# First batch of a chunked attention with a mixture of experts: two heads in one product, loads in halves, no limit on transfers, a new order

## The chip, the cores and the metric

The kernel runs on one core of one Trainium2 chip. The metric is the time of one execution on the device in microseconds (us); lower is better. A core has five engines, each with its own instruction stream: TensorE (PE; its weight loads are shown apart as PEld), VectorE (DVE), ScalarE (ACT), GpSimd (POOL) and SyncE (SP), which here only issues transfers between DRAM and the core's memory (SBUF). PE writes its results to PSUM.

## What is computed

```
for c in range(S // 32):                       # chunks of 32 queries
    ctx = positions 32*c-16 .. 32*c+40         # 16 to the left, 8 to the right, cut at the ends
    k_full = concat(mem_k, k[ctx]);  v_full = concat(mem_v, v[ctx])     # 8 memory keys
    a = softmax(q_c @ k_full.T / 8)
    out[c] = a @ v_full
x = out as (4*768, 512)
for e in range(4):
    y += p[:, e] * (relu(x @ w1[e]) @ w2[e])   # p: domain_probs, each row divided by its sum
```

There are 4 batches of 8 heads, 768 positions and 64 values a head. All is float32. A product of the experts is made of three products of split operands (a high part and a low remainder); a product of the attention is a plain float32 product.

## The kernel before, in words

A unit u is 96 queries (three chunks) of all 8 heads; a batch has 8 units. The first batch is worked before the experts can begin, since the first expert's first product needs x. Everything after it is one long stretch of expert products, with the attention of later units between them.

Units 0 to 3 of the first batch go one at a time, by these steps, whose names are used below:

- S: `early_scores` (L1411) loads `qk[u]` (128 rows of 3712 bytes: two heads by 64 values in the rows) and makes the scores. A product has 64 rows of contraction (one head), 32 queries and 64 keys. There are 24 of them a unit: 4 head pairs, 3 chunks and 2 heads of the pair (the `rows` slice, L531). The chunk chooses a strip of 32 columns of PE's array, the head one half of its rows. DVE then takes the maximum (L1426), subtracts it (L1456), and ACT takes the exponential (L607).
- T: `early_turn` transposes the result on PE in four transposes (L1499); the result is copied to `aTs` (two buffers).
- X: `early_values` loads `v0[u]` (128 rows of 3120 bytes) and multiplies, 24 products of 64 by 32 by 65 (L1520); the 65th column is the sum of the weights. DVE inverts it and multiplies (L1531 to L1535).
- Y: `early_mix` transposes the result (L1552), ACT copies the high part into `xa` (L603), DVE or POOL makes the low part.

Units 4 to 7 go in pairs: P4 and P6 (`early_pair`, L1476; two halves a and b on PE) and then X4 to X7. N0 to N7 are the first products of the first expert (`plain_first`, L931); each needs all of Y0 to Y3 and a weight block loaded from `w1`.

The order is written out by hand. `FIRST_BLOCK` makes the steps; `Plan.follow` puts their operations into the order of `FIRST_ORDER`, and every engine's stream is in that order. `MID_ORDER` and `FIN_ORDER` do the same for the rest. So an instruction that waits holds all behind it on its engine, SP's transfers too. W puts products of a zero tile (`idle`) at PE's start, and `still` puts some into planned gaps; they change nothing in the result. What comes ahead of the orders (zeroing `idle`, `low_band` and `turn`, and making `ident`, the matrix that the transposes need) is placed by the framework.

`start_transfer` (L630) limits the loads of the first batch: a load waits until the youngest load with at least `FLIGHT` (850,000) bytes issued behind it has landed. So the fourth load (S3) is issued when S0's has landed, the fifth (X0's values) when S1's has, the sixth when S2's has, and the eighth when S3's has.

Of the kernel before, what the change touches and what calls it, by code (L numbers as in the profile page):

```python
# [10 lines left out]
F32 = mybir.dt.float32  # L11
# [34 lines left out]
W32 S0 T0 S1 S2 T1 S3 X0 T2 X1 T3 X2 X3 Y2 Y3 Y0 Y1 P4 N0 N3 N2 X4 N7 N5 N6 N1 X5 N4 g2 P6 g1 g0 G1 G0 X7 X6 G2  # L46
# [3 lines left out]
1 0 9 e l q w 12 16 2y 2 3 3l a 4 5 2s b 6 f c 7 1q g d m 8 h j 1r n i r k o 5j u s p x v' 34 t 10 y 13 11 3x z 5k 14  # L50
17 2z' 15 4e 30' 3m' 18 1a 19 3f 1m 1b 1i 1c 2t' 1n 1e 3r 1j 1o 1d 1s 1f 1k 1g 48 2u' 1t 31 1u 1h 4n 3a 35 3n 1v 4j 36
3y 2v 32 1p 27 43 33 20 29 4r 3z' 1w 4z 1l 3g 37 4f 2w 57 3s' 3h 24 22 1z 5l 2x 38 1y 3t 3o 25 2a 49 4k 4v 39 21 53 23
4l 4s' 1x 5m 26 4m 3p 3i 4a 2b 3q 28 4o 5n 2c 4t' 5b 5o 3u 3j 2d' 5p 4u 3k 4b 3v 5c 3w 58' 2i 2e 50' 2j 2g 4p' 40 4c
2k 4d 4w' 4q 2l 54' 2h 4g 6q 41 4x' 2m 6r 42 2n 5f 2f 55' 4y 2o 5g 2p 60 5v 6m 4h' 59' 2q 56 5x 62 6n 51 4i 5s 5y 6o
5q 5a 5r 2r 52 6s 5z 5d 64 5u 6p 63 5e 5t 5h 5w 61 3b 65 66 6u 67 3c 74 3d 5i 3e 6c 44 6d 6v 45 6e 79 6w 68 7e 6f 6a
6t 6g 7f 69 6h 6z 6i 46 7g 6j 47 6x 6b 7h 6k 6y 6l 70 7i 7a 75 7b 7c 71 76 7d' 72 77 78' 7j 73
# [3 lines left out]
2 0 1q 1r 1 4 3 24 3n 3o 1s 5 1d x 1e 1i 8 1t 6 7 1k 1f y 1w b 1l 9 1y 1g 1u 11 a 2r 1h e 10 c d 1m 1v 15 h 1x f 1p t  # L60
z g 20 1z 12 u' k 22 i 1j 18 26 17 n l j 13 m v 14' 16 25 2s q 2v 1a o w 35 p 1c 2w' 2i 1b 21 r 19 1n 2j s 23 2y' 2z
2k 1o 33 2l 30' 2t 27' 2m 2n 36 2x' 2a 2o 28' 31 34 2p 2c 2b 32' 38 3b 29' 2q 2d 3c 6g' 2u 3d 6h 6j' 57 3e 3a 6i' 39
3f 37 3g 2e 3h 2f' 2g 3i 5b 3k 3j 2h 4o 3p 3m 3q 3l 4q 4p 3r 44 4u 4r 6c 4v 3w 6d 4s 4w 58 4t 6q 3t 4x 64 59 5c 4y 3s
3u 3v 5d 68 3x 50 4z 5a 3z 40 52 7h 51 5e 6k 53 41 6l' 54 42 43 46 55 47 65 6r 5f 56 66 69 5j 5g 6o 45 6a 6p 7l 3y 5l
5k 67 5h 5p 7i 8u 5i 7p 6b 5m 7j 5s 6t 48 5q 5n 5u 8y 5r 5t 49' 7k 5o 7m 5w 5v 60 6e 7n 6m 4e 5x 6w 8v 61 6n 5y 6y 6f'
9m 62 7q 6x 7o 7t 4f 72 6v 5z 6s 8z 6u 7w 75 73 63 83 7u 77 81 6z 76 74 70 90 79 82 78 7x 7d 7v 7r a0 71 86 7s' 89 7z
91 7e 92 7y 7f 8w 8b 88 8a 7a 87 4a 84 8f 7b 9o 8c 9n 8i 7c 8d 8x 8g 7g 8k 4g a2 8j 80 8m 4h 96 8l 85 8h 99 4i 8q 94
4c 4j c9 ae 4b 4k 9e af 8r 4l ag 8s 4d ah 4m 9p ai 8n 9s aj 9q 4n 8o 8e 9u ak 9t 8p an 9v al 9r' am ar ao cb 8t ap ca
au at aq 9w cn 9f 97' as 9x 9a bx 9y a1 98' ax by 9b 9j 9c ay 9z bz 93 9d' 9h 95 c0 c1 cg cd' 9g c2 cl az ce c3 9i ch
c4 cf cm b0 c6 b4 c5 cj 9l b1 c7 ci b3 9k b7 ct ck b9 cq ba c8 a3 cu bb co bc cc cv a6 a4' aw be a5 cw a7 bf b2 cx bd  # L70
b6 a8 cy b8 bg b5 cz bh a9 d0 bi d2 cp d1 bn d3 bl cs bo d4 db cr bp dd di d5 dc av d6 dn df' do' d7 bq en dg' d8 br
# [12 lines left out]
pb p8 s2 rw px p9 s3 pe pc rz tb pd pg rx pf pa sg s0' pi ph tx pm s1 pj q0 q8 q1 pk qi q9 qg t8 pn s6 qh qk pl po t9
pp qj r9 qm qe tc rb ra s7' s9' sa v4 s8' rf se rc sb' sf rd ri rg ty rh ta rk rj re qn td' rm rl sh qo ub rq tz' sc
# [1767 lines left out]
```

## Time and profile before

| | us |
|---|---|
| median of three runs | 1021.43 (1021.29 to 1022.74) |
| the profiled execution | 1021.78 |
| its span in the trace | 1020.0 |
| PE busy | 1011.6 (99%) |
| POOL busy | 544.5 (53%) |
| the first expert product begins at | 23.22 |

The span is the time from the first to the last instruction. A time in the rows below counts from the span's start. PE's ends are modelled and its instructions overlap, so the chain of waits, which counts each stretch once, is a better measure of how long a group took than the sum of its instructions. The granted clock (PEclk) is a share of 2.4 GHz.

### The profile page before, as it was taken

The numbers are of one execution on the slowest core, as the hardware profiler recorded it, in microseconds if no ns is written. First come the engines' busy times: TensorE is split into PE (matmuls) and PEld (weight loads), VectorE is DVE, ScalarE is ACT, GpSimd is POOL, SyncE is SP. The second block draws the span as 40 slices with busy tenths as digits, with TensorE's granted clock in tenths as the row PEclk, the third lists the DMA queues.
The fourth block names the chain that finished last, engine by engine and source line by source line (L and its number), as shares of the span: only waits on it lengthen the run. The fifth ranks groups of instructions, "written<-read, shape, count | busy, mean of one in ns | idle before, by whom it ended". The sixth has DMA issues, their size and how long they took to land.

```text
span 1020.0 us, 20660 instructions
## 1 busy us (share of the span) xinstructions
PE 1011.6 (99%) x7566; PEld 975.3 (96%) x7566; DVE 789.2 (77%) x1245; ACT 518.6 (51%) x1415; POOL 544.5 (53%) x478
## 2 busy tenths in 40 slices
PE   8999999999999999999999999999999999999998
PEld 6898989989899999999999999999999999999998
DVE  5685987988969869797899759678697756849385
ACT  3756755747546465445655554453544535343241
POOL 4654733555559454586465714354276655527263
PEclk9999999999999999999999999999999999999999
DMA  8869989979789899899998987888778887878784
GB/s 274 293 210 363 362 324 390 382 286 382 282 288 354 292 377 312 301 367 313 353 291 280 287 269 252 287 267 276 236 253 277 293 263 257 271 246 278 248 257 146
DMA packets 184644, 299.28 MB, mean 293 GB/s; under 512 B 11904, under 2 KB 126176, under 8 KB 184544
## 3 DMA queue, kind: packets, MB, share of 16 engines
q1 hardware_dynamic: 184544, 297.97, 85.4%
q8 instruction: 60, 0.98, 0.4%
q14 instruction: 40, 0.33, 0.1%
HBM read 228.66 MB, written 69.26 MB: 292 GB/s over the span
## 4 chain that ended last, share of the span: by engine, by line
PE 98%; DVE 1%; issue 0%; ACT 0%; POOL 0%; DVEq 0%; POOLq 0%
PE a_ps L999 24%; PE a_ps L1289 20%; PE moe_ps L999 18%; PE moe_ps L1289 15%; PE moe_ps L978 13%; PE moe_ps L931 3%; PE s_ps L736 1%; PE x_ps L758 1%; PE moe_ps L758 1%; PE x_ps L1385 1%; PE att_ps L531 0%; DVE u L1101 0%; PE att_ps L1520 0%; PE att_ps L1476 0%; PE x_ps L1565 0%
## 5 line engine op out<-in xcount | busy, mean ns | idle before, releaser
L978 PE MATMUL moe_ps<-w,h_hi 128*128 128x512 f32 x384 | 119.4, 392 | 0.0
L603 ACT CAST A_hi<-u 128x384 fp32r<-128x384 f32 x144 | 72.8, 515 | 59.0 <-DVE u L1101 42.0
L603 ACT COPY u<-a_ps 128x384 f32<-128x384 f32 x120 | 57.2, 476 | 87.2 <-PE a_ps L999 86.8
L622 POOL TENSOR_TENSOR A_lo<-u,A_hi 128x384 fp32r<-128x384 f32 x47 | 53.1, 1133 | 83.5 <-ACT A_hi L603 83.5
L621 DVE TENSOR_TENSOR u<-moe_ps,u 128x384 f32<-128x384 f32 x120 | 66.1, 551 | 40.4 <-PE moe_ps L999 28.2
L999 PE MATMUL a_ps<-xc_hi,w 128*128 128x384 f32 x432 | 92.3, 334 | 0.0
L621 DVE TENSOR_TENSOR A_lo<-u,A_hi 128x384 fp32r<-128x384 f32 x97 | 84.5, 879 | 9.7 <-ACT A_hi L603 9.2
L978 PEld LDWEIGHTS moe_ps<-w,h_hi 128*128 128x128 f32 x384 | 71.3, 188 | 15.0
L622 POOL TENSOR_TENSOR u<-u,routes 128x384 f32<-128x384 f32 x43 | 45.3, 1056 | 75.4 <-ACT u L605 75.3
L1289 PE MATMUL a_ps<-A_hi,w 128*128 128x384 f32 x320 | 81.6, 335 | 0.1
L999 PEld LDWEIGHTS a_ps<-xc_hi,w 128*128 128x128 f32 x432 | 76.5, 188 | 0.5
L978 PE MATMUL moe_ps<-w,h_lo 128*128 128x512 f32 x192 | 75.0, 390 | 0.0
L621 DVE TENSOR_TENSOR acc<-a_ps,acc 128x384 f32<-128x384 f32 x78 | 42.9, 550 | 37.5 <-PE a_ps L1289 36.9
L1101 DVE SCALAR_TENSOR_TENSOR u<-u,routes 128x384 f32<-128x384 f32 x72 | 64.9, 911 | 0.2
L622 POOL TENSOR_TENSOR raw<-raw 128x256 f32<-128x256 f32 x41 | 37.2, 908 | 51.1 <-DVE raw L621 34.8
L621 DVE TENSOR_TENSOR u<-a_ps,u 128x384 f32<-128x384 f32 x60 | 33.1, 552 | 32.6 <-PE a_ps L999 27.3
L1289 PEld LDWEIGHTS a_ps<-A_hi,w 128*128 128x128 f32 x320 | 57.6, 188 | 0.8 <-DVE u L1101 0.6
L605 ACT ACTIVATE u<-u 128x384 f32<-128x384 f32 x72 | 37.9, 527 | 39.1 <-DVE u L621 38.6
L693 ACT ACTIVATE s_pair<-s_ps,mx_two 96x64 f32<-96x64 f32 x192 | 57.4, 322 | 0.3
L622 POOL TENSOR_TENSOR us<-u,us 128x384 f32<-128x384 f32 x33 | 41.3, 1252 | 26.1 <-DVE us L621 25.6
L999 PE MATMUL a_ps<-xc_lo,w 128*128 128x384 f32 x216 | 54.9, 334 | 0.0
L1289 PE MATMUL a_ps<-A_lo,w 128*128 128x384 f32 x160 | 53.5, 334 | 0.0
(254 smaller groups left out, 3068.8 us busy)
## 6 DMA issues: line engine op xcount, KB each, us to landing
w<-k SPq DMA_DIRECT2D x126, 512.0 KB, 4.6
w<-w SPq DMA_DIRECT2D x96, 512.0 KB, 5.5
w<-t SPq DMA_DIRECT2D x84, 512.0 KB, 6.0
k<-w SPq DMA_DIRECT2D x48, 512.0 KB, 5.9
raw<-in_w_dram SPq DMA_DIRECT2D x62, 256.0 KB, 5.2
w<-k SPq DMA_DIRECT2D x38, 256.0 KB, 4.5
raw_pair<-in_w_dram SPq DMA_DIRECT2D x32, 256.0 KB, 5.4
t<-t_hi SPq DMA_DIRECT2D x32, 256.0 KB, 5.6
```

What stands on the lines that cost most here:

```text
L603: nc.scalar.copy(out(), x())
L605: nc.scalar.activation(out(), x(), func)
L621: ("DVE", t_dve(cols), lambda: nc.vector.tensor_tensor(out=out(), in0=x(), in1=y(), op=op)),
L622: ("POOL", t_pool(cols), lambda: nc.gpsimd.tensor_tensor(out=out(), in0=x(), in1=y(), op=op)),
L693: now["plan"].add("ACT", t_act(KW) + 0.147, lambda i=i, h=h, j=j, g=g: nc.scalar.activation(whole()[:, i * H + h, :], at()[0:UQ, j, i, g, ...
L736: nc.tensor.matmul(at()[c * CH:(c + 1) * CH, j, i, g, :], lhsT=x[rows, g * UQ + c * CH:g * UQ + (c + 1) * CH], rhs=x[rows, k0:k0 + KW], st ...
L758: nc.tensor.matmul(out[j * D:(j + 1) * D, g, :], lhsT=late_st[w]["v"].ap[:, h * D:(h + 1) * D], rhs=late_st[w]["aT"][:, j * NPAIR + g, :], ...
L931: nc.tensor.matmul(ps.ap[:, lo:hi], lhsT=a[:, c * P:(c + 1) * P], rhs=x[:, c, lo:hi], start=(i == 0), stop=(i == len(steps) - 1),)
L978: nc.tensor.matmul(self.ps.ap, lhsT=h.ap[:, self.rows], rhs=w.ap[:, part, :], start=(i == 0 and k == 0), stop=(i == NF - 1 and k == 2),)
L999: nc.tensor.matmul(ps.ap[:, 0:SG], lhsT=a()[:, c * P:(c + 1) * P], rhs=y[:, k0 + c, :], start=(first and i == 0), stop=(i == len(steps) - ...
L1101: dve(lambda: nc.vector.scalar_tensor_tensor(out=u.ap, in0=x(), scalar=0.0, in1=r.ap, op0=ALU.max, op1=ALU.mult), SG, [r], [u] + keys, two ...
L1289: nc.tensor.matmul(ps.ap[:, 0:SG], lhsT=w_ap[:, y, rows], rhs=x.ap, start=(begins and k == 0 and i == 0), stop=(k == NP2 - 1 and i == 2), ...
```

## The change

1. S and X of units 0 to 3 handle both heads of a pair in one product. The two heads' keys (values) lie in different rows and in different columns, with zeros in the other half of the rows, and the product has 128 rows of contraction and two blocks of 64 (65) columns: 12 products a unit instead of 24. The strips of 32 columns stay.
2. The zeros are written once, ahead of the order. The keys of units 0 and 1 lie in `pair_spots[0]` (zeroed by DVE), those of units 2 and 3 in `pair_spots[1]` (zeroed by POOL), and the values in four `v_spots` (zeroed by POOL, ahead of `pair_spots[1]` in the program). `low_band` goes from POOL to DVE; `minus`, which nothing used, goes.
3. Each load of S and X becomes two, of 64 rows each.
4. `start_transfer` and its limit go.
5. The products of zeros become float32, and W has 16 products (64 columns) in place of 32.
6. The three orders are new, and a few operations change engine. In names, the start of the streams:

```
PE before: W S0 S1 S2 T0 S3 T1 X0 T2 X1 T3 X2 X3 Y2 Y1 Y0 Y3 P4a P4b N3 N0 ...
PE after:  W S0 S1 S2 T0 S3 T1 X0 T2 X1 T3 X2 Y1 X3 Y2 Y0 P4a Y3 P4b P6a N0 N2 N5 N6 P6b ...
SP before: S0 S1 S2 S3 X0 X1 X2 X3 w1 w1 w1 P4a P4b w1 ...
SP after:  S0 S0 S1 S1 S2 S2 S3 S3 X0 X0 X1 X1 X2 P6a X2 X3 X3 w1 P4a P4b w1 ...
DVE after: ... S0.max S1.max S0.subtract S1.subtract S2.max ...
```

```diff
-FLIGHT = 850e3
...
-    def start_transfer(dst, src, bytes_):
-        ins = nc.sync.dma_start(dst, src).ins
...
-            if between >= FLIGHT:
-                tc.add_manual_dep(ins, older.name, mybir.DependencyInfo(
-                    mybir.DependencyClass.Sync, mybir.DependencyReason.DATA), reason="transfers under way")
...
-        now["plan"].add("SP", 0.1, lambda: start_transfer(dst(), src(), bytes_), reads, writes, bytes_=bytes_)
+        now["plan"].add("SP", 0.1, lambda: nc.sync.dma_start(dst(), src()), reads, writes, bytes_=bytes_)
...
-    idle = head.tile([P, P], mybir.dt.bfloat16, name="idle")
+    idle = head.tile([P, P], F32, name="idle")
...
-    nc.gpsimd.tensor_scalar_mul(minus, ident[0:UQ, 0:UQ], -1.0)
...
-    nc.gpsimd.memset(low_band, 0.0)
+    v_spots = [early.tile([P, 2 * VW], F32, name="v_e"), h_block().bitcast(F32)[:, 0:2 * VW],
+               head.tile([P, 2 * VW], F32, name="v_0"), head.tile([P, 2 * VW], F32, name="v_1")]
+    nc.vector.memset(low_band, 0.0)
     aT_pair = turn.rearrange("p (h q) -> p h q", h=2 * H)
     nc.gpsimd.memset(aT_pair, 0.0)
+    for spot in v_spots:
+        nc.gpsimd.memset(spot[0:D, VW:], 0.0)
+        nc.gpsimd.memset(spot[D:P, 0:VW], 0.0)
...
+    QW, KT = NPAIR * UQ, NPAIR * KEYS
+    XW = QW + 2 * KT
+    pair_spots = [head.tile([P, 2 * XW], F32, name="qk_pair"), h_block().bitcast(F32)[:, 0:2 * XW]]
+    for eng, spot in zip((nc.vector, nc.gpsimd), pair_spots):
+        both = spot.rearrange("p (i w) -> p i w", i=2)
+        eng.memset(both[0:D, :, XW - KT:], 0.0)
+        eng.memset(both[D:P, :, 0:KT], 0.0)
...
     def early_scores(u):
...
+        for j in range(2):
+            to, rows = i * XW + j * KT, slice(j * D, (j + 1) * D)
+            dma(lambda to=to, rows=rows: pair.ap[rows, to:to + QW + KT], lambda rows=rows: qk[u, rows], D * (QW + KT) * 4,
+                [], [(pair, 2 * i + j)])
...
+            for g in range(NPAIR):
+                for c in range(NCU):
+                    q0 = KT + g * UQ + c * CH
+                    nc.tensor.matmul(
+                        s_ps()[c * CH:(c + 1) * CH, 2 * g:2 * g + 2, :], lhsT=x[:, q0:q0 + CH],
+                        rhs=two(x, g * KEYS + STARTS[c], KT + QW, KW), start=True, stop=True,
+                    )
...
     def early_pair(u):
-        pair = new(lambda: head, [P, H * (UQ + KEYS)], "qk_pair", 2, parts=2)
+        k = 1 if u < 6 else 0
+        pair = homes[u // 2] = now["plan"].slot(f"qk_{k}", [pair_spots[k]], 4)
...
     def early_values(u):
...
-                    for j in range(2):
-                        rows = slice(j * D, (j + 1) * D)
...
+                    nc.tensor.matmul(
+                        o_ps()[c * CH:(c + 1) * CH, g, :].rearrange("p (j k) -> p j k", j=2),
+                        lhsT=aTs[u % 2][:, g, c * CH:(c + 1) * CH], rhs=two(t.ap, (c * NPAIR + g) * (D + 1), VW, D + 1),
+                        start=True, stop=True,
+                    )
```

Here D is 64, VW 780, KT 544 and QW 384. The hidden blocks of the experts come from four larger tiles instead of 32 small ones, since two of these first hold `v_spots[1]` and `pair_spots[1]`.

`two(x, at, step, cols)` is a view of two blocks of `cols` columns, `step` apart.

## Rows read from the trace of the kernel before

**Rows 1.** The page's first part: span, busy time and share of an engine, instructions.

```profile
span 1020.0 us, 20660 instructions
PE 1011.6 (99%) x7566; PEld 975.3 (96%) x7566; DVE 789.2 (77%) x1245; ACT 518.6 (51%) x1415; POOL 544.5 (53%) x478
```

**Rows 2.** Busy time by stretch: from:to, length, each engine's busy us (instructions), PEclk, DMA share, GB/s.

```profile
23.30:40.00 16.70, 16.70 (x182) 16.02 (x183) 11.55 (x21) 11.48 (x47) 11.88 (x12) 1.00 0.87 289
600.00:800.00 200.00, 199.87 (x1398) 198.29 (x1398) 154.36 (x241) 95.22 (x245) 99.75 (x83) 1.00 0.82 267
```

**Rows 3.** The chain that ended last, first 40 us: start, length, engine, output and line.

```profile
4.59 1.02 PE att_ps L531 x48
...
7.50 0.71 PE att_ps L531 x44
8.22 0.49 PE moe_ps L1499 x4
...
9.33 1.26 issue
...
14.27 1.49 issue
...
16.68 0.72 PE att_ps L1520 x45
...
21.26 0.90 issue
...
23.29 6.45 PE moe_ps L931 x36
29.73 0.67 PE att_ps L1476 x46
```

**Rows 4.** Busy time by stretch, between the ends of the stalls.

```profile
10.55:15.70 5.15, 3.52 (x126) 2.72 (x127) 3.75 (x9) 2.32 (x5) 0.27 (x1) 1.00 0.93 311
15.70:22.10 6.40, 5.50 (x127) 4.71 (x127) 3.61 (x9) 2.82 (x6) 3.85 (x4) 0.73 0.86 282
```

**Rows 5.** The page's DMA queues: packets, MB, share of 16 engines.

```profile
q8 instruction: 60, 0.98, 0.4%
```

**Rows 6.** Busy time by stretch: the one at a low clock.

```profile
17.20:20.60 3.40, 3.40 (x35) 3.10 (x24) 2.09 (x6) 1.72 (x4) 1.11 (x3) 0.50 0.93 328
```

**Rows 7.** SP's timeline, loads that waited for S0's and S3's: start, length.

```profile
4.03 0.33 SPq L631 DMA_DIRECT2D qk_pair<-in_qk_dram  x1
...
8.53 0.99 SPq L631 DMA_DIRECT2D w<-in_v_dram  x1
```

**Rows 8.** POOL's timeline: what stands ahead of the order, from the third memory write.

```profile
1.14 0.95 POOL L511 MEMSET s_pair<- 32x1024 f32 x1
2.14 1.38 POOL L513 MEMSET turn<- 128x1536 f32 x1
3.56 0.29 POOL masks.py:199 TENSOR_SCALAR_AFFINE_SELECT ident<-ident 128x128 f32<-128x128 f32 x1
3.94 0.45 POOL L506 TENSOR_SCALAR minus<-ident 96x96 f32<-96x96 f32 x1
```

**Rows 9.** DVE's timeline: S0's maximum and subtraction, X3's last step.

```profile
5.96 0.69 DVE L1426 TENSOR_REDUCE mx<-att_ps 96x8 f32<-96x512 f32 x1
6.68 0.69 DVE L1456 TENSOR_TENSOR s_pair<-att_ps,mx 96x512 f32<-96x512 f32 x1
...
18.09 0.69 DVE L1535 TENSOR_TENSOR spot<-att_ps,sm 96x512 f32<-96x512 f32 x1
```

**Rows 10.** ACT's timeline: S0's exponential, Y3's high part.

```profile
7.40 0.63 ACT L607 ACTIVATE s_pair<-s_pair 96x512 f32<-96x512 f32 x1 [5.38 <-DVE s_pair L1456]
...
21.06 0.48 ACT L603 CAST xa_hi<-x_ps 128x384 fp32r<-128x384 f32 x1 [0.62 <-PE x_ps L1552]
```

More of the change, by code (lines that the diff above doesn't have):

```diff
@@ L210 @@
 ASIDE = (0, 1, 2, 3, 4, 6, 7)
-MOVED = (0, 1, 7)
-FUSED = (5, 6, 7)
-APART = (0, 1, 3)
-LIFTED = ()
-LENT = (2, 4, 6)
-HIGH = (3, 4, 5, 6)
-LOW = (1, 4, 5, 7)
+MOVED = (0, 1, 5, 7)
+FUSED = (4, 5, 6, 7)
+LENT = (2, 4, 5, 6)
+HIGH = (2, 3, 5)
+LOW = (4, 5, 7)
 LOCK = 0.14
@@ L411, in emit @@
                     idle = op.end - op.time - busy - 0.1
-                    self.fill(max(0, int(FILLED * idle / (0.107 if busy < COLD else 0.06))))
+                    self.fill(max(0, int(FILLED * idle / (0.427 if busy < COLD else 0.214))))
                 busy = op.end
@@ L486, in tile_chunked_attention_moe, with h_block, more_hidden @@
     late = {}
+    def h_block():
+        return hpool.tile([P, NF * SG], F32R, name="h")
+    h_spots = [], []
+    def more_hidden():
+        for spots in h_spots:
+            block = h_block()
+            spots.extend(block[:, f * SG:(f + 1) * SG] for f in range(NF))
     def open_late():
         head_ctx.close()
+        more_hidden()
         xc.extend(in_parts(ctx.enter_context(tc.tile_pool(name="xcp", bufs=1, side="right")), "xc", 6))
@@ L576, in route @@
         nc.vector.tensor_tensor(out=pr, in0=pr, in1=psum_e.broadcast_to([P, NT, E]), op=ALU.mult)
-    now = {"plan": Plan({"PE": 0.9, "SP": 0.6, "ACT": 2.0, "DVE": 0.8, "POOL": 4.6}, rate=395e3, lands=(0.35, 1.9), lag=True)}
+    now = {"plan": Plan({"PE": 0.9, "SP": 0.6, "ACT": 2.0, "DVE": 4.2, "POOL": 11.7}, rate=395e3, lands=(0.1, 1.4), lag=True)}
     def new(pool, shape, name, bufs, dtype=F32, parts=1):
@@ L910, in hidden @@
     def hidden(n, f, half):
-        hid[n, f, half] = tuple(new(lambda: hpool, [P, SG], f"h_{part}", NF * 2, F32R) for part in ("hi", "lo"))
+        hid[n, f, half] = tuple(now["plan"].slot(f"h_{part}", h_spots[k]) for k, part in enumerate(("hi", "lo")))
         return hid[n, f, half]
@@ L1381, in tile_chunked_attention_moe, with still @@
     first = {}
-    def still(n):
+    def still(n, cols=P):
         for _ in range(n):
-            nc.tensor.matmul(x_bank[:, DM - P:DM], lhsT=idle, rhs=idle, start=True, stop=True)
+            nc.tensor.matmul(x_bank[:, DM - P:DM - P + cols], lhsT=idle, rhs=idle[:, 0:cols], start=True, stop=True)
     def zeros(n):
-        pe(0.107 * n, lambda: still(n), [], ["still"])
+        pe(0.2135 * n, lambda: still(n, P // 2), [], ["still"])
     def early_weights(which, f):
@@ L1406, in early_weights, with two @@
             dma(lambda: kept2("w2", 0, f // NH)[:, f % NH], lambda: t.ap.bitcast(F32), P * 2 * DM * 4, [t], [(2, 0, f)])
+    homes = {}
+    def two(x, at, step, cols):
+        one = x[:, at:at + cols]
+        return bass.AP(one.tensor, one.offset, [one.ap[0], [step, 2], [1, cols]])
     def early_scores(u):
@@ L1504, in early_values @@
     def early_values(u):
-        if u in APART:
-            t = new(lambda: w2pool, [P, 2, DM], "w2", 8, F32R, parts=2)
-            v_ap = lambda: t.ap.rearrange("p k d -> p (k d)")[:, 0:VW].bitcast(F32)
-        else:
-            t = now["plan"].slot("v_spot", v_spots)
-            v_ap = lambda: t.ap
-        dma(v_ap, lambda: v0[u], P * VW * 4, [], [t])
-        o_ps = new(lambda: ps_head, [P, H, P], "att_ps", 2)
+        t = now["plan"].slot(f"v_{u}", [v_spots[u]], 2)
+        for j in range(2):
+            rows = slice(j * D, (j + 1) * D)
+            dma(lambda j=j, rows=rows: t.ap[rows, j * VW:(j + 1) * VW], lambda rows=rows: v0[u, rows], D * VW * 4, [], [(t, j)])
+        o_two = new(lambda: ps_head, [P, H, P], "att_ps", 2)
+        o_ps = lambda: o_two.ap.rearrange("p h k -> p (h k)").rearrange("p (g w) -> p g w", g=NPAIR)[:, :, 0:2 * (D + 1)]
         def fn():
```

187 lines of the change are left out of this document (79 added, 108 removed).

## The prediction, as it was written before the kernel was run

> **What bounds the kernel now.** I read the page's first part, then busy time by stretch, the chain of waits, the timelines of the engines. TensorE is busy for 1011.6 of 1020.0 us [rows 1]. From its first expert product on it never stops: 16.70 of 16.70 us to 40, and in the loosest stretch after that 199.87 of 200 [rows 2]. So a change to the first batch is worth what it moves the start of that stretch (23.29 on the chain), less any work put ahead of it or behind it.
>
> Ahead of 23.29 the chain has three gaps marked "issue", where PE waited for nothing shown: 1.26 at 9.33, 1.49 at 14.27, 0.90 at 21.26 [rows 3], 3.65 us. Between their ends stand 126+127 and 127+127 matmuls and weight loads [rows 4]. Queue q8 brings "instruction" packets, 60 of them [rows 5]; PE's 7566 matmuls and as many loads [rows 1] make 252 a packet. So I read the gaps as PE out of instructions: a packet holds some 254, and the next came 5.15 and 6.40 us after the one before, while PE had used the old one up sooner. It is an inference, from the equal counts. After the second gap the clock was at 0.50, 1.2 GHz, for the 3.40 us from 17.20 [rows 6].
>
> **The product of two heads.** S2's 48 matmuls (24 products, each in two passes) took 0.71 at the full clock, S0's 1.02 before it [rows 3]. What PE did ahead of S0 was W alone, so I take S0's clock as half. Then the part that goes with the columns is 1.02 - 0.71 = 0.31 at full clock, and 0.40 is start and end. The change halves the instructions, doubles the columns of each, and gives up the two row halves that ran side by side; the three strips stay. So each strip streams twice the columns: 0.40 + 0.62 = 1.02, against 0.71, and 0.40 + 1.24 = 1.64 at half clock. Bounds: 0.36, if the count of instructions sets the time, and 1.42, twice 0.71. I take 1.02, the only one that follows the difference between two rows. X has 65 columns and took 0.72 [rows 3]: the same. That adds 0.3 to each of six and 0.6 to S0 and most of S1: PE gets longer, not shorter.
>
> **The zeros.** POOL's row shows 0.95 us for 1024 columns, on 32 rows, and 1.38 for 1536, on 128 [rows 8]: 0.84 ns a column and 0.09, whatever the rows. The eight writes of 780 columns take 0.75 each, 6.0; the two of 1088 take 1.0 each, 2.0. POOL ended its first work at 4.39; 0.95 (`low_band`) and 0.45 (`minus`) go: 4.39 - 1.40 + 8.0 = 11.0. The writes of `pair_spots[1]` are last in the program, and POOL took its memory writes in program order, with `ident`'s selection, which depends on one, behind them. So S2, which reads `pair_spots[1]`, cannot begin before 11.0, where it began at 7.50 [rows 3]. Behind it on PE wait T0, S3 and all else; behind T0, ACT and DVE. Ends: 7.6 (no hold) and 12.5 (POOL slowed by DVE's writes beside it). I take 11.0. DVE's own zeros are 1024 + 2 x 1088 columns. No row shows such a write on DVE; at POOL's rate they take 2.8, at the 0.69 for 512 of [rows 9] 4.3, so they end between 3.7 and 5.2, and S0 begins at 4.6 to 5.2. S2's wait hides that.
>
> **The clock.** PE will stand from 7.6 to 11.0, longer than both gaps before the low stretch of [rows 6] together. I charge one such stretch of 3.4 us in which PE does half its work: 1.7. Ends: 0 and 3.4 (two).
>
> **The sum, from 11.0.** PE's order to X3 has six products of 1.02 (S2 S3 X0 X1 X2 X3) and five transposes of 0.49 [rows 3] (T0 T1 T2 T3 Y1): 8.6, and 1.7 for the clock: X3 ends at 21.3. DVE's inversion and multiplication must follow before Y3: in the trace X3 ended at 17.40 (16.68 + 0.72) [rows 3] and the multiplication at 18.78 [rows 9], 1.4. So Y3 begins at 22.7; Y2, Y0 and P4a stand in that gap. Then Y3 0.49, P4b 0.67, P6a 0.67 [rows 3]: N0 at 24.5. Y3's high copy of 0.48 [rows 10] lies beside P4b. P6a stood behind the first N before (29.73), so 0.67 is work done early: 24.5 - 0.67 - 23.29 = 0.5. The three gaps are already out of this sum. One may remain: a unit's S or X has 48 matmul and load instructions in place of 96, so 384 fewer, and of the boundaries every 256, one falls near X2 and the next at P4b or P6a, some 4 us later, where the trace had 5.15 and 6.40 from one packet to the next. I charge 0.4; ends 0 and 2. Sum: +0.9. Own range -1.2 to +4.2, with clock and packet both at their low or high ends.
>
> Costed at nothing: the new orders behind N0 (PE is never without work there; if that cover fails, each late operand shows as a gap, and the loosest stretch had 0.13), the changed engines of a few copies, `minus`, and W, which runs while S0's load is on its way (it lands at 4.03 [rows 7]): if the float32 W lasts longer, S0 is late by that, and S2's wait hides it. If the hold on S2 falls, W and S0 are next on the path.
>
> **Loads.** S3's load was issued at 4.03, when S0's had landed, and X3's at 8.53, when S3's had [rows 7]: three loads of 464 KB in 4.5 us, 1.5 each. Without a limit the queue is never empty. At that rate, and with 2.5 us ahead of the first byte (4.03 less 1.5), S3 lands at 8.5, X0's and X1's values (390 KB, 1.27 each) at 11.0, X2's, with P6a's keys between its halves, at 13.8, X3's at 15.1, a weight block of 256 KB at 15.9, P4's two at 18.9; P4b needs the last at 23.2 in the sum. So halves cost nothing unless they run slower. No row has a load of 64 rows; ends: a factor f of 1 and of 2 on the 11.1 us of halved loads (4 x 1.5 + 4 x 1.27). I take 1, the rate of the 128-row loads: the same bytes in rows of the same length. But P4's keys go where S2's and S3's lay, so SP waits for S3 with them; at 11.0 + 1.02 + 0.49 + 1.02 + 1.0 (slow clock) = 14.5 that is no later than the queue.
>
> The Trainium skill speaks against this ("SBUF — State Buffer", section "Door 1: The DMA port swizzle (why `[64,N]` ≈ `[32,N]`)"): rows 0 to 63 reach only half of the memory's ports, rows 64 to 127 the other half, and two loads, one on each, hardly gain over one. It measured 196 GB/s on 64 rows where 128 had 328, a factor of 1.67. By that the time would be 1025.1 (an estimate, with that page's ratio as the f of rival 2 below); by the rows at f = 1, 1022.3. No run here shows it so far.
>
> **Rivals.** (1) S2 isn't held: the zeros come earlier, or their order is another. For it: POOL's only other duty ahead of them is `ident`. Against it: 8.0 us of writes at the rate of [rows 8], these last. Then S0 ends at 6.2, S1 at 7.6 (the clock full on the way, as S2's 0.71 at 7.50 shows); with S1's maximum now ahead of S0's subtraction, S0's exponential ends at 7.6 + 0.15 + 0.69 + 0.69 + 0.63 = 9.8 [rows 9, 10]. From T0: four transposes and Y1, 2.45, and S3 to X3, five of 1.02: 17.4; Y3 at 18.8, N0 at 20.6, and with the 0.4 for the packet 21.0: 21.0 - 0.67 - 23.29 = -3.0. That is 1018.4.
>
> (2) Slower: each half load takes f times its share. N0 can't begin before P4's second load has landed and P4b and P6a are done: 2.5 + 11.1 f for these, 5.3 for the whole loads among them (three of 1.5, one of 0.8), and 1.34. It decides from f = 1.4, where this passes 24.5; at 2 it gives 31.3, +7.4. Midway, 1.7, it is 28.0, +4.1, 1025.5. For it: 64 rows is the only new thing in these loads. Against it: nothing in the trace.
>
> (3) The change doesn't rid PE of the gaps: with up to twice the bytes under way the packets come later still, and two gaps of 1 to 1.5 remain where I charge 0.4: +2.5 more, about 1024.5. For it: the waits of 5.15 and 6.40 under a limit. Against it: half the instructions in S and X.
>
> **Numbers.** The working stands against the profiled 1021.78 (span 1020.0 and 1.78 around it), 0.35 above the median of the three runs, 1021.43; so 1022.7 there is 1022.3 as a median. Chances: forecast 0.43, rival 1 0.26, rival 2 0.22, rival 3 0.09. What a measurement can tell from no change is 0.2%, 2.0 us. Of the forecast, 0.33 falls inside that, 0.02 below and 0.08 above; of rival 1, 0.03 inside and 0.23 below; of rival 2, 0.05 inside and 0.17 above; of rival 3, 0.02 and 0.07. Faster 0.25, no change 0.43, slower 0.32. The range takes rival 1 with a margin of 0.8 for a smaller packet gap, and the upper side to where rival 2 is past its middle: 1017.6 to 1025.8; the forecast's own is 1020.2 to 1025.6.
>
> **What would show it.** S2 on PE beginning at 11 with POOL's write of `pair_spots[1]` as releaser; an S or X at 1.0 at full clock with 24 matmuls; no gap "issue" at 9 and 14; a low clock between 10 and 17; the first L931 product near 24.5 behind P6a. S2 at 7.6 makes rival 1 right; PE waiting for halves of X2 or X3, landing later than 16, rival 2; "issue" gaps over 1 us, rival 3. The forecast is wrong in kind if the first expert product stays within 0.5 of these marks and the time still moves, as then PE's long stretch isn't the cover that I take it for.

## The result, and the profile after

The changed kernel takes 1027.8 us (median of 4 runs, 1027.08 to 1029.48) where the kernel before took 1021.36 (4 runs, 1020.89 to 1022.74). The ratio is 1.0063, 95% interval 1.0046 to 1.0081: slower by 0.6%, more than the 0.2% that can be told from no change. The forecast was 1022.3, no change, and its range ended at 1025.8, so the time lies outside.

The page's first part, beside [rows 1], and its line of instruction packets, beside [rows 5]:

```profile
span 1027.7 us, 20284 instructions
PE 1018.7 (99%) x7361; PEld 981.4 (95%) x7361; DVE 794.9 (77%) x1261; ACT 517.0 (50%) x1417; POOL 534.9 (52%) x471
...
q8 instruction: 58, 0.95, 0.4%
```

PE has 205 matmuls fewer and is busy 7.1 us longer. The chain of waits of the changed kernel to the first expert products (start, length, engine, output and line), beside [rows 3]:

```profile
1.00 7.09 PE x_ps L1387 x32
8.09 3.57 PE att_ps L1434 x48
11.66 1.24 PE x_ps L1387 x6
12.90 0.32 issue
13.21 1.07 PE att_ps L1434 x24
...
19.50 0.79 PE att_ps L1520 x17
20.29 1.03 issue
21.32 0.49 PE att_ps L1520 x7
...
22.29 1.02 PE att_ps L1520 x24
...
25.29 0.47 PE att_ps L1481 x32
25.76 2.25 issue
28.01 0.91 PE att_ps L1481 x54
28.92 10.10 PE moe_ps L933 x48
```

The first row is W (L1387), which was over at 4.59 before. The second is S0 and S1, 1.78 each, where the same 24 instructions take 1.00 to 1.07 later: PE is at 1.2 GHz until S1 is done. Then S2 at 13.21, two stalls "issue" of 1.03 and 2.25, and the first expert product at 28.92 instead of 23.29. The 48 matmuls behind it take 10.10; before, 36 took 6.45 [rows 3] and the next 12 2.31. Busy time by stretch, columns as in [rows 2]:

```profile
5.00:10.00 5.00, 5.00 (x45) 4.68 (x47) 0.00 (x0) 0.00 (x0) 4.71 (x8) 1.00 1.03 232
10.00:15.00 5.00, 4.68 (x67) 3.72 (x64) 3.40 (x6) 1.43 (x3) 1.00 (x1) 1.00 1.05 225
...
20.00:25.00 5.00, 3.97 (x102) 2.95 (x97) 2.77 (x9) 2.17 (x5) 1.53 (x2) 1.00 1.05 396
25.00:30.00 5.00, 2.75 (x105) 2.38 (x104) 4.61 (x6) 2.34 (x7) 4.26 (x5) 0.95 1.05 388
30.00:35.00 5.00, 5.00 (x22) 5.00 (x22) 3.80 (x8) 3.54 (x19) 4.13 (x5) 0.71 0.63 205
```

Two things are to be seen. The queues are full throughout (share 1.03 to 1.05), yet move 225 to 232 GB/s while the halves of 64 rows come in and 388 to 396 once whole loads follow. And the granted clock is at 0.71 when the expert products begin: the low stretch that the prediction put at 10 to 17 lies on them. (The granted clock reads 1.00 from 5 to 10 although S0 ran at half speed: the trace's first entry for the clock is its rise to 1.00, at 12.40 here and 6.94 before, and the view shows 1.00 ahead of it too. For the start, that entry and the length of one shape at two places are the better witnesses.)

The account of this execution: the first expert product 5.63 later, less 0.67 for P6a, now done ahead of it; 1.34 for the low clock on the products (10.10 less 8.76); 0.9 for two waits of the next stage on DVE, which PE had not had. Together 7.2 of the 7.7 us between the spans. (This execution, 1029.48, was the longest of the four; the medians are 6.4 us apart.)

```profile
PE a_ps L1001 <- DVE u L638: 0.6, 1, 0.6
...
PE a_ps L1001 <- DVE h L1079: 0.3, 1, 0.3
```

These are from the list of what PE waited for in the changed kernel (total, times, longest).

### The profile page after: what moved, and what is told of

Its sections match the earlier page's. It is cut to its first block, busy times and chain, and to the rows that moved or that the text cites. A ratio compares the mean times of both kernels' runs of the same rounds, so it can differ in the third digit from the quotient of the medians.

```text
span 1027.7 us, 20284 instructions
## 1 busy us (share of the span) xinstructions
PE 1018.7 (99%) x7361; PEld 981.4 (95%) x7361; DVE 794.9 (77%) x1261; ACT 517.0 (50%) x1417; POOL 534.9 (52%) x471
## 4 chain that ended last, share of the span: by engine, by line
PE 95%; DVE 2%; issue 1%; ACT 1%; DMA 1%; POOL 0%; POOLq 0%; DVEq 0%
PE a_ps L1001 22%; PE a_ps L1291 19%; PE moe_ps L1001 17%; PE moe_ps L1291 15%; PE moe_ps L980 13%; PE moe_ps L933 3%; PE s_ps L738 1%; PE x_ps L760 1%; PE x_ps L1387 1%; PE moe_ps L760 1%; PE att_ps L1434 1%; DMA raw<-in_w_dram 1%; DVE u L638 0%; PE att_ps L1520 0%; DVE u L1103 0%
## 5 line engine op out<-in xcount | busy, mean ns | idle before, releaser
L980 PE MATMUL moe_ps<-w,h 128*128 128x512 f32 x576 | 134.9, 391 | 0.0
L980 PEld LDWEIGHTS moe_ps<-w,h 128*128 128x128 f32 x576 | 107.4, 188 | 22.5
L638 DVE TENSOR_TENSOR acc<-moe_ps,acc 128x384 f32<-128x384 f32 x66 | 36.1, 549 | 21.1 <-PE moe_ps L1291 20.8
```

What stands on the lines that cost most here:

```text
L638: ("DVE", t_dve(cols), lambda: nc.vector.tensor_tensor(out=out(), in0=x(), in1=y(), op=op)),
L980: nc.tensor.matmul(self.ps.ap, lhsT=h.ap[:, self.rows], rhs=w.ap[:, part, :], start=(i == 0 and k == 0), stop=(i == NF - 1 and k == 2),)
```

## Experiments

All runs in one table; below the first line, which is the result, each was timed beside the kernel before on the same chip. The median of that kernel lay between 1021.06 and 1021.85 there, so the ratios are to be compared, not the medians. "Filler" is what W and the fillers between stages are made of. The kernels with full-height loads leave out the second head's block, so they compute other numbers with products of the same sizes; whether the values matter to the time was not tried.

| kernel | median us | ratio to before, 95% |
|---|---|---|
| changed | 1027.80 | 1.0063 (1.0046–1.0081) |
| changed, bfloat16 filler | 1028.50 | 1.0066 (1.0053–1.0078) |
| changed, full-height loads | 1025.98 | 1.0042 (1.0030–1.0054) |
| changed, both | 1023.94 | 1.0021 (1.0011–1.0032) |
| changed, both, keys' zeros first | 1021.89 | 1.0002 (0.9993–1.0011) |
| the same, with the limit | 1023.71 | 1.0016 (1.0006–1.0025) |
| changed, both, P6a later, DVE's order | 1025.21 | 1.0035 (1.0023–1.0047) |
| changed, bfloat16 filler, keys' zeros first, halves on two queues | 1026.25 | 1.0045 (1.0032–1.0058) |
| changed, with the limit | 1027.82 | 1.0059 (1.0046–1.0071) |
| changed, P6a later | 1029.07 | 1.0071 (1.0057–1.0084) |
| changed, P4b and P6a later | 1031.62 | 1.0096 (1.0082–1.0110) |
| before, float32 filler | 1025.96 | 1.0046 (1.0031–1.0061) |
| before, float32 filler, half of W | 1022.51 | 1.0006 (0.9997–1.0014) |
| before, bfloat16 W twice as long | 1026.61 | 1.0051 (1.0038–1.0065) |
| before, loads in halves | 1025.46 | 1.0036 (1.0023–1.0049) |
| before, no limit | 1023.15 | 1.0016 (1.0008–1.0025) |
| before, fewer instructions | 1022.20 | 1.0012 (1.0003–1.0021) |

### The filler and the loads, undone one at a time in the changed kernel

```diff
-W16 S0 S1 S2 ...
+W32 S0 S1 S2 ...
...
-                    self.fill(max(0, int(FILLED * idle / (0.427 if busy < COLD else 0.214))))
+                    self.fill(max(0, int(FILLED * idle / (0.107 if busy < COLD else 0.06))))
...
-    idle = head.tile([P, P], F32, name="idle")
+    idle = head.tile([P, P], mybir.dt.bfloat16, name="idle")
...
-        pe(0.2135 * n, lambda: still(n, P // 2), [], ["still"])
+        pe(0.107 * n, lambda: still(n), [], ["still"])
```

Expected: 

> Theory A (the filler): W in float32 took 7.09 us where the bfloat16 W of before took 3.60, and the clock rose at 12.4 instead of 7.0, so S0 and S1 ran at half clock. With the bfloat16 filler back, W ends near 5, S0 begins when its halves land (5 to 6), the clock is full before S1 ends, S2 begins at 11.0 (end of the zeros) instead of 13.21, and the low stretch no longer falls on the first expert products: 2.2 to 4 us less than the changed kernel, 1023.5 to 1025.6. Theory B (filler beside the point: S2 is held by the order on DVE and by the zeros, and the rest by loads): 0 to 1 us less, 1026.8 or more.

Measured: 1028.5, no gain. My theory that the filler explains most of the loss fell in this form. What PE waited for, with the bfloat16 filler:

```profile
PE att_ps L1481 <- issue: 2.8, 1, 2.8
PE att_ps L1520 <- DMA v<-in_v_dram: 2.0, 1, 2.0
PE att_ps L1434 <- DMA qk_pair<-in_qk_dram: 1.9, 2, 1.1
```

The time that W gave back went to waits for the halves: 1.9 for S0's and S1's, 2.0 for X2's.

```diff
-            dma(lambda to=to, rows=rows: pair.ap[rows, to:to + QW + KT], lambda rows=rows: qk[u, rows], D * (QW + KT) * 4,
-                [], [(pair, 2 * i + j)])
+            if j == (0, 1, 1, 1)[u]:
+                dma(lambda: pair.ap[:, i * XW:i * XW + QW + KT], lambda: qk[u], P * (QW + KT) * 4,
+                    [], [(pair, 2 * i), (pair, 2 * i + 1)])
...
```

The values are loaded the same way, and the zeros of the lower rows' blocks move to the second block.

Expected: 

> The changed kernel with each unit's keys and values brought by one load of 128 rows into the first block instead of two of 64 rows; the second head's block is then not where the product reads it, so the scores are other numbers, while every product, zero and copy keeps its size. Row halves as a cause of the slow loads: the rate before 20 us goes from 230 GB/s to 300 or more and a 3712-byte packet from 258 ns to about 145. Theory A, where PE does not wait for these loads: the time stays within 0.7 us of the changed kernel. If the loads set the start of the experts (rival 2 of the prediction): 3 us or more less, 1024.8 or under.

Measured: 1025.98, between the two expectations. In the ratio it is 0.2% better than the changed kernel, about as much as the two intervals can tell apart. The stretch from 5 to 10, the same bytes in 128 rows:

```profile
5.00:10.00 5.00, 5.00 (x45) 4.68 (x47) 0.00 (x0) 0.00 (x0) 4.72 (x7) 1.00 0.99 391
```

391 GB/s against 232, at a busy share of 0.99 against 1.03: the engines are no busier, the packets are slower (a packet of 3712 bytes took 255 ns in the median between 3 and 20 us, here 145, as in the kernel before). But S2 began no earlier than in the changed kernel (the chain of waits with full-height loads):

```profile
8.09 3.60 PE att_ps L1437 x48
...
11.71 0.69 DVE mx L1454
12.40 0.61 DVE s_pair L1464
13.01 0.25 issue
13.26 1.07 PE att_ps L1437 x24
```

S1 ends at 11.7, DVE takes its maximum first, and S0's subtraction, which frees the bank that S2 writes, comes after that. The gain lies behind, and not in waits for loads, of which PE had none in the changed kernel either. The first of the two stalls is gone, as its packet of instructions set out at 14.76 instead of 18.45 (why sooner isn't shown), and the clock doesn't fall on the expert products:

```profile
24.34 2.53 issue
...
27.76 8.52 PE moe_ps L933 x48
```

### Both, and the zeros

Expected, of both: 

> The changed kernel with both the bfloat16 filler and the loads of 128 rows (the second head's block then holds other numbers; sizes are the same). Alone, the filler gave nothing (with W out of the way PE waited 2.0 us for X2's halves) and the full-height loads 1.8 us. Theory C (two walls, one behind the other, W to 8.1 and the halves to 19.3): together S2 begins at 11.0, when the zeros end, the first expert product about 2 us earlier than with full-height loads alone (27.76), and the time falls below both: 1022.5 to 1024.5. Theory D (PE is bound by its packets of 256 instructions, each some 7 us after the last, whatever stands ahead): within 0.7 us of full height alone, 1025.3 to 1026.7.

Measured: 1023.94, below either. In the ratio the single effects are 0.0021 and -0.0003, the joint one is 0.0042: that is how two covers over one another look. (Each of these is uncertain by some 0.002, so the ratios alone do not show it; that PE waits for the halves only with W out of the way does.) The chain now goes through POOL, as the prediction had it:

```profile
8.96 1.00 POOL h L568
...
10.00 1.01 POOL h L569
...
11.05 1.07 PE att_ps L1437 x24
```

So the zeros were the third wall. The first expert product begins at 23.64 by the timeline. The next kernel writes the keys' zeros first:

```diff
-    for spot in v_spots:
-        nc.gpsimd.memset(spot[0:D, VW:], 0.0)
...
     for eng, spot in zip((nc.vector, nc.gpsimd), pair_spots):
...
+    for spot in v_spots:
+        nc.gpsimd.memset(spot[0:D, VW:], 0.0)
...
```

Expected: 

> The kernel with bfloat16 filler and full-height loads (other numbers in the second block), and the zeros of the keys' blocks written on POOL ahead of the values' zeros. With filler and loads out of the way S2 stood still from 8.98 to 11.05 for these zeros. Theory E (the zeros are the third wall): S2 begins at 9.0 to 9.8, behind S0's subtraction, and the first expert product 1.2 to 2 us earlier than with the zeros last: 1021.8 to 1023. If something else sets the end by now: 1023.5 or more.

Measured: 1021.89, ratio 1.0002: the whole loss is gone. S2 begins at 8.11 and the first expert product at 21.19 (the chain of waits of this kernel):

```profile
8.11 1.07 PE att_ps L1437 x24
...
19.56 0.65 issue
...
21.19 8.53 PE moe_ps L933 x48
```

This execution took 1019.39 and was the fastest of eleven, which reach to 1023.88, so its places are likely earlier than those of a middling one. S2 still begins behind a write of zeros on POOL, now one of the values', over at 7.91.

### The same causes, put into the kernel before

```diff
-W32 S0 T0 S1 ...
+W16 S0 T0 S1 ...
...
-    idle = head.tile([P, P], mybir.dt.bfloat16, name="idle")
+    idle = head.tile([P, P], F32, name="idle")
...
-        pe(0.107 * n, lambda: still(n), [], ["still"])
+        pe(0.2135 * n, lambda: still(n, P // 2), [], ["still"])
```

Expected: 

> The kernel before with the changed kernel's float32 filler alone (W16 of 64 columns, and the fillers between the stages). Theory A: W lasts to about 8, S0 and S1 run at half clock, the chain to the first expert product is 2.5 to 4 us longer: 1024 to 1025.5. Theory B: S0 to T0 had slack, at most 1 us: 1021.4 to 1022.4.

Measured: 1025.96, a little above the range of theory A. W takes 7.09 here too, and the transposes behind it 0.83 instead of 0.49 [rows 3]; the clock's rise is entered at 19.32:

```profile
0.99 7.09 PE x_ps L1385 x32
...
12.05 0.83 PE moe_ps L1499 x4
```

The first expert product is 3.4 us later than before (26.70 against 23.29). From S2 to X1 the steps took about 2.6 us longer than before, where the clock was full, so the low clock behind W is a large part of it here.

Whether the length of W costs, or a clock that this filler doesn't raise, was tried with half of it (W8), and with the old filler twice as long (W64).

```diff
-W32 S0 T0 S1 ...        # bfloat16
+W8 S0 T0 S1 ...         # float32, the first
+W64 S0 T0 S1 ...        # bfloat16, the second
```

Expected, of the short float32 filler: 

> The kernel before with the float32 filler as in the run that cost 4.7 us (W16: 7.09 us, and transposes at 0.83 instead of 0.48 us until 18), but with half of W (W8), so that W lasts 3.5 us as the bfloat16 W does. If the length of W is what costs: within 0.7 us of before, 1020.7 to 1022.2. If the float32 filler leaves TensorE at half clock whatever its length: the transposes stay at 0.83 for 10 us or more and it costs 2 to 4 us: 1023.4 to 1025.5.

Expected, of the long bfloat16 filler: 

> The kernel before with its own bfloat16 filler, twice as long (W64: 6.8 us at half clock, less if the clock rises on the way). If length costs: S0 begins 2 to 3 us later, 1023 to 1024.5. If the clock is what the float32 filler costs: the clock is full from about 7, S0 and S1 run in 0.71 each, and the time is 1021 to 1022.5.

Measured: 1022.51, ratio 1.0006 (0.9997 to 1.0014), for the short one. Fillers followed its W, so that PE's zeros lasted to 6.05; S0 ran at half clock and S1 at full (its rise is entered at 7.23), and the transposes take about 0.5:

```profile
0.99 5.06 PE x_ps L1385 x22
```

The long bfloat16 one took 1026.61, ratio 1.0051 (1.0038 to 1.0065). So a float32 filler does not keep the clock down whatever its length. Nor does W cost from the moment when S0's load has landed (4.03, [rows 7]): 2.0 us beyond that, with S0 1.5 late, cost nothing that can be told, 4.0 us beyond it cost 0.46%. The result of the long bfloat16 one is beyond what I had expected for length alone: S0 began 2.03 late, and four stalls "issue" followed, 0.99, 2.18, 2.04 and 1.31, where before had three of 3.65 in all; 32 more products in W had moved the ends of the packets. That run mixes the two. What kept the clock low behind the long float32 W is not shown. In the six kernels with it the rise is entered at 9.8 to 19.3, always behind W's end at 8.1; with the bfloat16 W of before it is at 3.7 to 7.0 in eight kernels and at 12.5 in one.

```diff
-        now["plan"].add("SP", 0.1, lambda: start_transfer(dst(), src(), bytes_), reads, writes, bytes_=bytes_)
...
+            for k in range(n):
+                rows = slice(k * D, (k + 1) * D) if n > 1 else slice(None)
+                start_transfer(dst()[rows] if n > 1 else dst(), src()[rows] if n > 1 else src(), bytes_ // n)
...
```

Expected: 

> The kernel before with each load of the first batch's keys and values issued as two of 64 rows, nothing else. If 64 rows run at 230 GB/s where 128 run at 300 to 325, X2's and X3's values land near 18 to 20 instead of ahead of 15.8, PE waits for them and the first expert product moves from 23.29 to 25.5 to 27: 1023.5 to 1025. If the halves are slow only in the changed kernel's pattern (two blocks, no limit): 1021 to 1022.5.

Here n is 2 for these loads. Measured: 1025.46, ratio 1.0036, a little above the range expected. The halves cost without blocks, zeros or filler. The path was not the one expected: PE waited for none of X2's and X3's halves, but 1.7 us for S0's to S2's and 0.3 for P4's; the clock was at 0.50 from 8.2 to 21.8; and the first expert product came 1.93 later (23.22 before, by the timeline).

```profile
5.00:10.00 5.00, 3.38 (x128) 2.40 (x133) 2.92 (x5) 0.78 (x2) 0.00 (x0) 0.82 1.04 241
10.00:15.00 5.00, 4.62 (x138) 3.60 (x132) 2.75 (x4) 2.08 (x5) 0.00 (x0) 0.50 1.03 240
```

From the timeline:

```profile
25.15 1.68 PE L936 MATMUL moe_ps<-xa_hi,w 128*128 128x384 f32 x8
```

### Is it one half of the rows at a time?

```diff
-                [], [(pair, 2 * i + j)])
+                [], [(pair, 2 * i + j)], nc.scalar if j else nc.sync)
...
```

The values' loads change in the same way; the filler is bfloat16 and the keys' zeros come first.

Expected: 

> The changed kernel, as it computes, with the bfloat16 filler, the keys' zeros first, and the upper 64 rows of each unit issued from ACT's queue while SP issues the lower 64. If a half is slow because only one half of the rows is being written at a time, the two queues together come to 320 GB/s or more ahead of 15 us and the time to that of full-height loads with the same filler, 1022 to 1024. If the halves stay at 225 to 260 GB/s: 1026.5 or more.

Measured: 1026.25. The same stretches move 250 and 259 GB/s, where one queue with this filler moved 236 and 227:

```profile
5.00:10.00 5.00, 3.91 (x50) 3.13 (x51) 0.86 (x3) 0.98 (x1) 4.66 (x8) 1.00 1.02 250
10.00:15.00 5.00, 4.96 (x72) 4.09 (x74) 3.65 (x6) 2.47 (x5) 1.01 (x2) 1.00 1.04 259
```

A second queue does not mend it.

### The limit on transfers

```diff
+FLIGHT = 850e3
...
-        now["plan"].add("SP", 0.1, lambda: nc.sync.dma_start(dst(), src()), reads, writes, bytes_=bytes_)
+        now["plan"].add("SP", 0.1, lambda: start_transfer(dst(), src(), bytes_), reads, writes, bytes_=bytes_)
```

In the kernel before, the other way:

```diff
-FLIGHT = 850e3
+FLIGHT = 850e9
```

Expected, of the changed kernel with the limit: 

> The changed kernel with the limit of 850 KB under way put back. If unlimited transfers make the instruction packets late (the gaps marked issue, 3.28 us on the chain), the packets take 0.9 us again instead of 1.1 to 1.3 and the gaps shrink to 2 or less: 1 to 2 us less, 1026 to 1027. If the gaps come from the count of instructions and not from the load on the queue: within 0.5 us of the changed kernel, or up to 2 us more because the halved loads (230 GB/s) then also start later.

Expected, of the kernel before without: 

> The kernel before with the limit on bytes under way taken off, nothing else. If unlimited transfers delay the packets of instructions (rival 3 of the prediction): the stalls ahead of the experts grow from 3.65 us to 5 or more, 1022.7 to 1024. If not: within 0.7 us of before, 1020.7 to 1022.2.

Expected, of the kernel with three causes undone (filler, loads, the place of the zeros), with the limit: 

> The kernel with bfloat16 filler, full-height loads (other numbers in the second block) and the keys' zeros first, with the limit of 850 KB under way put back: what is left of the change is the product of two heads, the zeros and the new orders. Taking the limit off cost the kernel before 1.6 us. If it costs the same here: 1.6 us less than without the limit (1021.9), 1019.8 to 1020.8, a little under before. If the limit matters only with the order of before: 1021.2 to 1022.5.

Measured: no difference in the changed kernel (1027.82); 0.16% slower in the kernel before, whose first two stalls grow (2.36 and 1.90, against 1.26 and 1.49):

```profile
9.32 2.36 issue
...
15.97 1.90 issue
```

The third is gone, so that they come to 4.26 in all against 3.65, and the clock was at 0.50 from 13.8 to 24.0, three times as long as before.

In the last, the limit doesn't help, and 1023.71 lies above both ranges expected (ratio 1.0016 against 1.0002 without it, the intervals overlapping a little). Its stall was 1.1 us, against 0.65, and PE waited another 1.0 behind its first expert products for operands (DVE's `h` and POOL's `w`), which it had not without the limit. The limit gains something with the order of before and nothing with the new one; taking it off is no cause of the loss here.

### The stalls "issue"

Wherever a stall "issue" of over 0.9 us comes, in these eighteen kernels, it stands behind the same counts of TensorE's instructions, 256 apart (449, 705, 961 and once 1217, matmuls and weight loads counted together), whatever work is there. Two experiments moved work past them.

```diff
-PE:  P4a Y3 P4b P6a N0 N2 N5 N6 P6b ...
+PE:  P4a Y3 P4b N0 N2 N5 P6a N6 P6b ...       (the first)
+PE:  P4a Y3 N0 N2 P4b N5 P6a N6 P6b ...       (the second)
```

Expected, with P6a behind the third expert product: 

> The changed kernel with P6a put behind the third expert product on PE, where the kernel before has it. In all six traces so far PE's stalls without a releaser end at its 449th, 705th or 961st matmul or weight load. With 92 of these out of the way the 705th falls among the expert products, 12 matmuls of which last over 2 us. Theory D: the stall of 2.25 us ahead of the first expert product is gone; it begins near 26 instead of 28.92, P6a costs its 0.67 later, and the low clock on the expert products may go too: 1.5 to 3.8 us less, 1024.0 to 1026.3. If the stall just moves to another place ahead of the experts: 1027 or more.

Expected, with P4b too: 

> The changed kernel with P4b (and the part of its softmax that stood ahead of it) put behind the second expert product on PE, and P6a behind the third. P6a alone gave nothing, since the 705th matmul or weight load lies inside P4b, ahead of it: the stall stayed (1.82 us). Now the 705th comes behind two expert products, which last 4.3 us. Theory D (the stall is the time by which PE reaches the end of a packet before the next one is there): the stall of 2.25 us goes, the first expert product begins at 25.5 to 26.5, less 1.34 us for P4b and P6a done later: 0.7 to 2 us less than the changed kernel, 1025.8 to 1027. If the stall has another cause at this place in the program, it moves with P4b and the time stays at 1027.5 or more.

Measured: 1029.07 and 1031.62, both no better than the changed kernel, the second 0.3% worse. In the first the stall stayed (1.82), as it lies ahead of P6a; the expectation had overlooked that. In the second it went, as theory D has it, and nothing was gained. What then held the first expert product is in its chain:

```profile
24.13 1.39 DVE xa_lo L638
25.52 0.94 DVE xa_lo L1580 x2
26.51 2.24 PE x_ps L1387 x10
```

DVE makes the last operands until 26.5, and then five float32 fillers (ten instructions), put where the planner expected idle time, take 2.24 on the path. In the changed kernel the same DVE steps end at 27.04 (its timeline):

```profile
24.72 1.39 DVE L638 TENSOR_TENSOR xa_lo<-xr,xa_hi 128x384 fp32r<-128x384 f32 x1 [0.19 <-ACT xr L620]
26.04 0.54 DVE L1580 TENSOR_TENSOR xa_lo<-moe_ps,xa_hi 128x384 fp32r<-128x384 f32 x1
26.50 0.54 DVE L1580 TENSOR_TENSOR xa_lo<-x_ps,xa_hi 128x384 fp32r<-128x384 f32 x1
```

So of the 2.25 us at 25.76 about 1.3 lie beside DVE's work. Whether that work would have held the first expert product is not shown: `plain_first` takes the low parts in the last four of its twelve matmuls, and what waited for DVE above were the fillers, which write a bank that DVE reads. The step of 1.39 us is Y2's low part, by what it reads, which the new order moved from POOL to DVE.

A last try was to make a better kernel of the one before, by fewer instructions ahead of the experts.

```diff
-W32 S0 T0 S1 ...        # a product has 128 columns
+W8 S0 T0 S1 ...         # 512 columns
...
-COLD, FILLED = 6.5, 0.9
+COLD, FILLED = 6.5, 0.0
...
-PE:  P4a P4b N3 N0
+PE:  P4a N3 P4b N0
```

Expected: 

> The kernel before with W as 8 products of 512 columns in place of 32 of 128, no fillers between the stages, and P4b behind the first expert product: 90 matmuls and weight loads fewer and 92 later ahead of the experts, so that the 961st falls among these and the stall of 0.90 us there goes. Theory D: 0.5 to 1.5 us less than before if the clock holds, 1020 to 1021; without the fillers the clock may fall, then 1022 to 1023.5.

Measured: 1022.2, ratio 1.0012 (1.0003 to 1.0021), in the range given for a falling clock. The stall at the 961st did go, and the one at the 705th grew from 1.49 to the first line here:

```profile
13.98 2.30 issue
...
20.00:25.00 5.00, 5.00 (x65) 4.42 (x63) 1.63 (x3) 1.70 (x4) 5.00 (x5) 0.59 0.90 283
```

PE came there 0.3 us sooner than before, while the packet that it waited for set out at the same time (13.48 against 13.44) and took 1.36 us instead of 0.92. A stall that ends when a packet comes is not shortened by getting there sooner. Even so the first expert product began at 21.71, 1.5 us ahead of before, with P4b (0.67) still to do. The rest went to the clock (second line, by stretch): it was at 0.50 from 17.25 to 24.07, twice as long as before, and the first twelve matmuls of the experts took 3.36 us where before 36 took 6.45 [rows 3].

Four edits were undone at once, with the zeros still last: filler, loads, P6a, and DVE's order:

```diff
-DVE:  S0.max S1.max S0.sub S1.sub
+DVE:  S0.max S0.sub S1.max S1.sub
```

Expected: 

> The changed kernel with bfloat16 filler, full-height loads (other numbers in the second block), S0's subtraction ahead of S1's maximum on DVE, and P6a behind the third expert product. If these are the causes, the first expert product begins at 22 to 23.5, as in the kernel before (23.29): 1020 to 1022. If another cause remains (the new orders behind the first expert product, the fewer buffers): 1023 or more.

Measured: 1025.21, ratio 1.0035 (1.0023 to 1.0047), and the first expert product at 25.74 by the timeline, not 22 to 23.5. It is no better than with filler and loads alone (1.0021). PE stood for 3.3 us waiting for the zeros, and S2 and S3 behind that took 1.70 and 1.59, at half clock. Whether the two further edits cost by themselves is not settled.

No version was found that beats both kernels. The one that loses nothing, 1.0002, holds other numbers in its second head's blocks; a way to fill these at the rate of 128 rows was not tried.

## Why the prediction was wrong

What PE's bound is, and that only the start of the long stretch counts, held: 5.63 - 0.67 + 1.34 of the loss is its start and its clock. The steps:

- **Loads at f = 1: failed.** "So halves cost nothing unless they run slower", and of the factor, "I take 1, the rate of the 128-row loads". They run at 232 where the old loads without a limit reach 388 and the full-height ones 391: a factor of 1.67 to 1.69; against the limited rate from which the sum was made (311, [rows 4]) it is 1.3 to 1.4, just where rival 2 said that it begins to decide, so that its formula gives next to nothing for it. In the changed kernel itself PE waited for no load, as W and S1 were later still; with W out of the way it waited 1.9 and 2.0 us for halves. Alone, in the kernel before, the halves cost 0.36%. The Trainium skill's rule ("SBUF — State Buffer", section "Door 1: The DMA port swizzle (why `[64,N]` ≈ `[32,N]`)") had 1.67, and the trace agrees in the ratio, though both rates are higher here than its 196 and 328 GB/s; its statement that a load on the other half beside the first hardly adds (section "Can I just issue two DMAs to hit both halves?") is borne out too, by 250 to 259 from two queues against 227 to 236 from one. I had weighed it against an absence of rows, and let the absence win.
- **W at nothing: failed.** "if the float32 W lasts longer, S0 is late by that, and S2's wait hides it". W lasts 7.09 against 3.60, each of its 32 instructions 0.22, and S0 and S1 are behind it at half clock. The diff's own estimate was 0.2135 for one product; a product is two of these instructions. So S1 ended at 11.66, past the 11.0 that was to hide it. In the kernel before the float32 filler alone cost 0.46%.
- **S2 held until 11.0 by the zeros: right in its place and size, not in its rank.** POOL ended at 11.0 to the tenth. But in the changed kernel S2 was held to 13.21 by S0's subtraction, behind S1's maximum on DVE, behind S1 on PE. The wall stood in sight when filler and loads were taken away (11.05), and its removal was worth 0.2%. Rival 1 gave the kernel without the hold its first expert product at 21.0; with all three walls gone it came at 21.19, in an execution of 1019.39 where rival 1 has 1018.4. The median there is 1021.89, so the time of rival 1 was not reached as a rule.
- **Clock, 1.7 on the way to X3: a size near the truth by luck, in the wrong place.** PE did not stand from 7.6 to 11.0, as W and S1 filled that time. The low stretch came behind the last stall, on the expert products, 1.34, and S0 and S1 at half clock cost 1.5 more.
- **Packets, 0.4: mis-sized.** The stalls on the chain are 3.60 us, where before had 3.65; two of over 1 us remain, as in rival 3, though not for its reason, as the limit changed nothing here.
- **The product of two heads, 1.02 at full and 1.64 at half clock:** 1.00 to 1.07 and 1.78. Right, and so the change lengthens PE's work, as said.
- **The orders behind the first expert product, at nothing:** two waits of 0.9 in all were there.

What failed as a whole is the way of adding. Each new cost was compared with one wall at 11.0 and dropped as hidden. There were three walls, W and S1 with DVE (13.0), the halves (X2's landed at 19.3 with W out of the way) and the zeros (11.0), so near to each other that each hid the next, and each later than the old path. Rival 2 with 0.22 and rival 3 with 0.09 were each a part of the outcome; no case had them together.

## What to carry to other kernels

When several new costs are each called hidden by the same wait, work out the finish of each as if the others were gone, and take the latest; an edit that undoes one of them will then show nothing, which is no proof that it is harmless: undo them together. A price that only the Trainium skill states, such as that of a load on half the rows, should move the forecast where no row speaks against it. And a filler that is there to warm an engine can itself become the path (here 1.5 us of delay stayed hidden and 3.5 us did not), so its own duration is to be taken from a measured instruction, not from the comment or the planner's estimate.

## What the runs showed of the hardware

- Loads of 64 rows (3712 or 3120 bytes in each) move 225 to 241 GB/s at a busy share of 1.02 to 1.06; loads of 128 rows move 388 to 404 at 0.99 to 1.04 (kernel before without the limit, changed kernel with full-height loads). Issuing the two halves from two queues gives 250 to 259.
- TensorE stops at the end of a packet of 256 of its instructions if the next isn't there. A packet's own transfer mostly takes 0.9 to 1.5 us, and where PE stalled it went on 2.2 to 2.9 us after that transfer began (3.7 once, where it took 2.4); in the changed kernel the transfers began at 18.45 and 25.49 and PE went on at 21.32 and 28.01. From crossing one such end to going on at the next it was 4.3 to 7.5 us where PE stalled. What makes a transfer begin is not known.
- A float32 filler of 64 columns takes 0.44 us at half clock (7.09 over 16, two instructions each), a bfloat16 one of 128 columns 0.11 (3.60 over 32): four times as long for half the columns. At full clock the bfloat16 one takes 0.056 (the long W from 5.0 on, where the rise is entered).
- The view's granted clock can read 1.00 ahead of its first entry while one shape takes 0.83 there and 0.48 later (the transposes of the kernel before with the float32 filler, first entry 19.32). After stalls it can fall to 0.50 for 3.4 to 10.2 us, and for 13.7 in the kernel before with halves, but not after every one: the kernel with full-height loads stood for 2.5 us at 24.3 and its next 48 products took 8.52, at full clock.
